# Top-k attention and Fourier mixing on one core: the second pair's q loaded before the tables and transposed in the third step

## The chip, the core and the metric

The kernel runs on one core of one Trainium2 chip. The core has five engines that run side by side, each through its own queue of instructions: TensorE (PE; its weight loads are shown apart as PEld), VectorE (DVE), ScalarE (ACT), GpSimd (POOL) and SyncE (SP), which here only issues transfers. The metric is the device time of one execution in microseconds, as a median over runs. A lower time is better.

## What is computed

Eight batches, each with eight heads of 576 rows and 64 channels. For each row of q the scores against all keys are formed, only the 32 largest are kept, and a softmax over these weighs v. The heads are put side by side to rows of 512 channels, a two-dimensional Fourier transform is added (its real part), the rows are normalised, and a two-layer MLP with a hidden width of 2048 is added.

```python
scores = scale * np.matmul(q, k.transpose(0, 1, 3, 2))
kth = np.partition(scores, -top_k, axis=-1)[..., -top_k:-top_k + 1]
attn = softmax(np.where(scores >= kth, scores, -1e9))
x = heads_side_by_side(np.matmul(attn, v))
u = x + np.real(fft(fft(x, axis=1), axis=2))
un = (u - mean(u)) / np.sqrt(var(u) + 1e-6)
out = u + np.maximum(un @ w_ch1, 0.0) @ w_ch2
```

## The kernel before

Two heads of one batch make a pair; there are 32 pairs, four for each batch. The rows of a pair are cut into nine tiles (four row blocks for each head, and one tile with the tails of both heads), so that there are 288 tiles, numbered 0 to 287, and 36 for a batch. The main loop (line 1049) makes one step for each tile. The order of the instructions on each engine is the order in which this Python program emits them; [...] each engine works through its own list.

In step i the loop emits, for the first batch:

- ACT conversion of a weight chunk (`scale_high`, line 171, and `rest`, lines 187 and 190). The weights arrive in a 64-bit form, 32 chunks of 512 KB, into five slots of one space, and are turned into 32-bit values by ACT, by DVE (`shift`, line 178) and by POOL (`join`, lines 197 and 198). Chunk n is converted in step n+1 (from chunk 16 on one step later), and the load of chunk n+5 into the slot that came free is issued by SP in the same step (line 165).
- ACT's exponent of tile i-1 (`expo`, line 390).
- PE's scores for the tiles ahead (`scores`, lines 346 and 316; ACT copies them to S at lines 349 and 320). A step handles the main part for two tiles or the tail part.
- In two steps of a pair's nine, the preparation of the next pair: `prep("q", ...)` or `prep("k", ...)`, five transposes on PE (line 260), and ACT copies to qT (268) or kT (270, 274). The natural rows come from `load_nat`, eight transfers issued by SP (lines 214 and 230: four of 64 KB and four of 8 KB).
- PE's transposes of tile i-1 (line 411 and, for its tail part, 422 or 426), which ACT copies to PT (414, 423), and for some tiles the product with v (448).
- DVE's search: four rounds of MAX8 (line 367) with three MATCH_REPLACE8 (369) for each tile. Step i does the last two rounds of tile i and the first two of tile i+1.
- POOL's threshold of tile i (`bounds`, line 376), ACT's mask (383), and POOL's subtraction (384). ACT's mask of tile i stands behind the PT copies of tile i-1 in ACT's list.
- DVE's shift of the weight chunk, then POOL's join of it.

q and k of all pairs but the first k share one buffer, `nat_t`. So the q of pair 1 may be loaded only when the q of pair 0 has been transposed, and the k of pair 1 only when the q of pair 1 has been. In the kernel before, q is prepared in the first step of a pair (i % 9 == 0) and k in the sixth (i % 9 == 5); the load of k follows in the step of q's preparation, and the load of the next q in that of k's.

Ahead of the loop, in this order, stand: the loads of the first q and k, the transposes of the first two row blocks of q and of all of k (lines 874 and 875), the loads of three weight chunks and of v, of the Fourier tables fs, fd and sg (895 to 897), of two more weight chunks, then the scores of tiles 0 and 1, the rest of the first q's transposes, the load of the second pair's q, and the scores of tiles 2 and 3. The tail part of tiles 2 and 3 is emitted there and again in step 0, with the same values.

From the second batch on, the MLP of the batch before fills PE beside the attention. The first batch has no such work beside it.

Of the kernel before, what the change touches and what calls it, by code (L numbers as in the profile page):

```python
# [64 lines left out]
def kernel(  # L65
# [15 lines left out]
    NC = 5  # L81
    NF = NC - 1
# [136 lines left out]
    def load_full(dst, src, pair):  # L219
        for e in range(2):  # L220
            for h in range(2):
                load_half(dst, src, pair, e, h)

    def load_tails(dst, src, pair, row0=(0, 0), queue=None, heads=(0, 1)):
        b, hp = divmod(pair, NPB)
        for e in heads:
            s2 = src[b, 2 * hp + e].rearrange("(h r) d -> h r d", h=2)
            for h in range(2):
                r0 = row0[e] + TH * h
                (queue or nc.sync).dma_start(  # L230
                    out=dst[r0:r0 + TH, NF, e, :], in_=s2[h, 2 * P:HS, :]
                )

    def load_nat(n, pair):
        if pair < NPAIR:
            nat[n, pair] = nat_t
            src = q if n == "q" else k
            load_full(nat[n, pair], src, pair)
            load_tails(nat[n, pair], src, pair)

    def load_v(pair):
        if pair < NPAIR:
            v_of[pair] = v_t[pair % 2]
            load_full(v_of[pair], v, pair)
            load_tails(v_of[pair], v, pair, (0, TAIL))

    def prep(n, pair, blocks=((0, NF), (NF, NC))):

        if pair >= NPAIR:
            return 0.0  # L250
        src, got_of = nat[n, pair], qT_of if n == "q" else kT_of
        if pair not in got_of:
            got_of[pair] = attp.tile(
                [P, S if n == "q" else NF * P], F32, name=f"{n}T_{pair}", tag=f"{n}T"
            )
        t_sb = got_of[pair]
        for c0, c1 in blocks:
            tp = ps_t.tile([P, 4, P], F32, name=f"tp{n}_{pair}_{c0}", tag="tp")
            for c in range(c0, c1):
                nc.tensor.transpose(  # L260
                    tp[:, c - c0, :], src[:, c, :, :].rearrange("p h d -> p (h d)"), ident
                )
            if c0 < NF:
                dst, got = t_sb[:, c0 * P:c1 * P], tp.rearrange("p a c -> p (a c)")[:, 0:(c1 - c0) * P]
            else:
                dst, got = t_sb[:, NF * P:], tp[:, 0, 0:TAIL]
            if n == "q":
                nc.scalar.mul(out=dst, in_=got, mul=scale)
            elif c0 < NF:
                nc.scalar.copy(out=dst, in_=got)  # L270
            else:
                for e in range(2):
                    r = slice(D * e, D * (e + 1))
                    nc.scalar.copy(out=kt_t[r, TAIL * e:TAIL * (e + 1)], in_=tp[r, 0, 0:TAIL])
        return 0.7
# [3 lines left out]
    PER_PAIR = len(IN_PAIR)  # L279
# [4 lines left out]
    N = len(items)  # L284
# [588 lines left out]
    nc.gpsimd.memset(ftail, 0.0)  # L873
    prep("q", 0, ((0, 2),))
    prep("k", 0)


    plan, costs, arrivals = {}, {}, []
# [11 lines left out]
    AHEAD = 5  # L890
    load, scale_high, shift, rest, join = weight_steps(wcs, sp1, WC, AHEAD)
    for n in range(3):
        load(n)
    load_v(0)
    nc.sync.dma_start(out=fs, in_=fs_d.ap())
    nc.sync.dma_start(out=fd, in_=fd_d.ap())
    nc.sync.dma_start(out=sg, in_=sg_d.ap())
    for n in range(3, AHEAD):
        load(n)
    start_of = [0] + [34 * n // len(wcs) for n in range(1, len(wcs))]  # L900
    for n, s0 in enumerate(start_of):
        at(s0 + 1, "convert", lambda n=n: scale_high(n))
# [121 lines left out]
    def run(i, where):  # L1024
        for fn in plan.pop((i, where), []):
            fn()
# [10 lines left out]
            got += one_unit()  # L1037
        return got

    for c in range(2):  # L1040
        scores(0, c)
    prep("q", 0, ((2, NF), (NF, NC)))
    load_nat("q", 1)
    for c in range(2):
        scores(2, c)
    for op in top_ops(0, (0, 1)):
        op()
    i, carry = 0, 0.0
    while i < N + 4 or plan or queue:
        now[0] = i  # L1050
        run(i, "begin")
        pair_of = i // PER_PAIR

        short = 0 <= i - 1 < PER_BATCH
        done = i - 1 if short else i - 2 if PER_BATCH <= i - 2 < N else None

        fixed, j = [], i + 3
        e = items[j][2] if j < N else None  # L1060
        preps = []
        if i < N and i % PER_PAIR == 0:
            preps.append(lambda: prep("q", pair_of + 1))
        if i < N and i % PER_PAIR == 5:
            preps.append(lambda: prep("k", pair_of + 1))
        fixed.append(lambda: scores(j - 1, 1) if e == 1 else scores(j, 0))
        n_mask = 0
        fixed += preps

        tok = []  # L1070
        if pending and pending[0][0] <= i:
            _, pp, pc = pending[0]
            if pp // NPB < 2 or pp // NPB - 2 in written:
                pending.pop(0)
                tok.append(lambda: to_tokens(pp, pc, not short))
        if not short:
            fixed += tok
        for where in ("pe1", "pe2", "pe"):
            fixed += plan.pop((i, where), [])
        if e is None and j < N:  # L1080
            fixed.append(lambda: scores(j, 1))
        n_tr = len(fixed)
        if done is not None:
            fixed.append(lambda: transposes(done))
        if short:
            fixed += tok
            pair, r = divmod(i - 1, PER_PAIR)
            piece = {1: (0, 0, P), 4: (0, P, CW[0]), 6: (1, 0, P), 8: (1, P, CW[1])}.get(r)
            if piece is not None:
                fixed.append(lambda: attend(pair, *piece))  # L1090
            if i == PER_BATCH:
                fixed.append(lambda: attended(NPB - 1, 1, late_next) or 0.0)
                fixed.append(lambda: to_tokens(NPB - 1, 1, False))
        if i in arrivals:
            carry = min(carry, 0.0) if i > arrivals[0] else -5.0
            run(i, "units")
            step_us = level(i)
        room = step_us - carry - fixed_cost(i)
        cost, got = carry, 0.0
        run(i, "convert")  # L1100
        if short:
            expo(i - 1)
        for n, fn in enumerate(fixed):
            cost += fn()
            if n == n_mask:
                if PER_BATCH <= i - 1 < N:
                    mask(i - 1)
                run(i, "act")
                for fn in out_next:
                    fn()  # L1110
                out_next.clear()
            if n == min(n_tr, len(fixed) - 1) and PER_BATCH <= i - 1 < N:
                expo(i - 1)

            got += some(max(room * (n + 1) / len(fixed) - got, 1.1 if fn in preps else 0.0))
        if short:
            if piece is not None and r in (4, 8) and i < PER_BATCH:

                out_next.append(lambda pc=(pair, r // 8): attended(*pc, late_next))
                pending.append((i + 1, pair, r // 8))  # L1120

        soon_tile = 2 * PER_BATCH - 1
        for tile in (i - 3, i - 2):
            if not PER_BATCH <= tile < N or (tile == i - 2) != (tile == soon_tile):
                continue
            pair, r = divmod(tile, PER_PAIR)
            if r in (4, 8):
                cost += attend(pair, r // 8)
                attended(pair, r // 8, late_next)
                pending.append((i + 1, pair, r // 8))  # L1130
        if i < N:
            if i % PER_PAIR == 0:
                load_nat("k", pair_of + 1)
            if i % PER_PAIR == 5:
                load_nat("q", pair_of + 2)
            if i % PER_PAIR == 6:
                load_v(pair_of + 1)
        first, second = top_ops(i, (2, 3)), top_ops(i + 1, (0, 1))
        for n in range(max(len(first), len(second))):
            for ops in (first, second):  # L1140
                if n < len(ops):
                    ops[n]()

        run(i, "pool0")
        bounds(i)
        if i < PER_BATCH:
            mask(i)
        for fn in late_now:
            fn()
        run(i, "dve")  # L1150
        for where in ("pool", "pool2", "load", "load2"):
            run(i, where)
        late_now[:] = late_next
        late_next.clear()
        carry = max(-4.0, min(4.0, cost + got - step_us))
        i += 1
# [36 lines left out]
```

## Time and profile before

| What | us |
|---|---|
| median of 8 runs | 1950.57 |
| lowest and highest of them | 1949.25 and 1951.54 |
| the profiled execution | 1950.67 |
| its span, from the first to the last instruction | 1948.9 |
| PE busy | 1826.7 (94%) |
| DVE busy | 1577.8 (81%) |
| ACT busy | 1202.8 (62%) |
| POOL busy | 773.9 (40%) |

The busy times are sums over the whole span. They hide that the kernel has stages: the page's row of 40 slices, 48.7 us each, has PE at 4 to 7 tenths in the first five slices and at 9 from the eighth on, and DVE at 9 or more in the second to the fourth. So the first 250 us have to be read by themselves. The granted clock of TensorE is a mean of 0.968 over the span, and 7 tenths in the first five slices.

In a line of the timeline, the first two numbers are the start and the length, in us; the bracket at its end tells how long the engine had been idle, and what ended the wait. SPq is SP's own queue: what is shown there is the issue of a transfer and not the transfer.

### The profile page before, as it was taken

The numbers are of one execution on the slowest core, as the hardware profiler recorded it, in microseconds if no ns is written. First come the engines' busy times: TensorE is split into PE (matmuls) and PEld (weight loads), VectorE is DVE, ScalarE is ACT, GpSimd is POOL, SyncE is SP. The second block draws the span as 40 slices with busy tenths as digits, with TensorE's granted clock in tenths as the row PEclk, the third lists the DMA queues.
The fourth block names the chain that finished last, engine by engine and source line by source line (L and its number), as shares of the span: only waits on it lengthen the run. The fifth ranks groups of instructions, "written<-read, shape, count | busy, mean of one in ns | idle before, by whom it ended". The sixth has DMA issues, their size and how long they took to land.

```text
span 1948.9 us, 27231 instructions
## 1 busy us (share of the span) xinstructions
PE 1826.7 (94%) x8626; PEld 1120.9 (58%) x8626; DVE 1577.8 (81%) x3245; ACT 1202.8 (62%) x3062; POOL 773.9 (40%) x1054
## 2 busy tenths in 40 slices
PE   4666699999999999999999999999999999998999
PEld 2443365464664756556664756556664756566655
DVE  7999989999999999888888879988888879843000
ACT  5878657776776767666666657666666657541100
POOL 3768642335523454235523444235522444232000
PEclk7777799999999999999999999999999999999999
DMA  4333100100001010010101100010001100000000
GB/s 144 108 94 106 29 13 20 32 20 24 23 16 29 21 30 13 19 33 19 24 19 25 27 22 18 16 32 19 24 19 25 27 22 20 1 14 1 11 14 11
DMA packets 133583, 57.80 MB, mean 30 GB/s; under 512 B 124352, under 2 KB 124480, under 8 KB 133440
## 3 DMA queue, kind: packets, MB, share of 16 engines
q1 hardware_dynamic: 132656, 55.85, 10.8%
q8 instruction: 69, 1.13, 0.3%
q14 instruction: 74, 0.61, 0.1%
q10 hardware_dynamic: 784, 0.21, 0.0%
HBM read 46.57 MB, written 9.44 MB: 29 GB/s over the span
## 4 chain that ended last, share of the span: by engine, by line
PE 78%; POOL 9%; DVE 5%; issue 4%; ACT 2%; DMA 1%; SPq 0%; ACTq 0%; POOLq 0%; DVEq 0%
PE hp L742 24%; PE cp L766 22%; PE o L448 7%; PE tpP L411 5%; PE sp L346 5%; POOL wk L384 3%; PE yp L607 3%; PE cp L802 3%; PE mp L656 2%; POOL w L198 2%; POOL w L197 2%; DVE m L367 2%; PE sp_t L316 2%; DVE wk L369 2%; PE tpq L260 1%
## 5 line engine op out<-in xcount | busy, mean ns | idle before, releaser
L384 POOL TENSOR_TENSOR wk<-S,wk 128x576 f32<-128x576 f32 x288 | 407.4, 1414 | 920.9 <-ACT wk L383 873.1
L367 DVE MAX8 m<-wk 128x8 f32<-128x576 f32 x864 | 623.3, 749 | 5.5
L742 PE MATMUL hp<-unT,w 128*128 128x256 f32 (+1 forms) x2048 | 538.8, 410 | 3.1 <-ACT unT L723 2.1
L766 PE MATMUL cp<-w,hT 128*128 128x512 f32 x1024 | 477.2, 597 | 0.0
L742 PEld LDWEIGHTS hp<-unT,w 128*128 128x128 f32 x2048 | 373.5, 191 | 126.1 <-issue 31.2
L369 DVE MATCH_REPLACE8 wk<-m,wk 128x576 f32<-128x576 f32 x576 | 427.5, 742 | 0.0
L766 PEld LDWEIGHTS cp<-w,hT 128*128 128x128 f32 x1024 | 179.4, 190 | 180.5 <-issue 179.9
L390 ACT ACTIVATE wk<-wk,nt 128x576 f32<-128x576 f32 x288 | 224.8, 781 | 53.6 <-POOL wk L384 52.7
L411 PE MATMUL tpP<-ident,wk 128*128 128x128 f32 x1152 | 183.9, 284 | 68.6 <-ACT wk L390 46.2
L414 ACT COPY PT<-tpP 128x512 f32<-128x512 f32 (+1 forms) x320 | 171.5, 548 | 117.9 <-PE tpP L411 115.5
L383 ACT ACTIVATE wk<-S,nt 128x576 f32<-128x576 f32 x288 | 227.0, 788 | 26.5 <-POOL nt L376 25.2
L411 PEld LDWEIGHTS tpP<-ident,wk 128*128 128x128 f32 x1152 | 139.9, 145 | 164.8 <-ACT wk L390 67.0
L746 ACT ACTIVATE hT<-hp 128x320 f32<-128x320 f32 (+1 forms) x256 | 104.9, 410 | 194.4 <-PE hp L742 192.0
L367 DVE MAX8 m<-S 128x8 f32<-128x576 f32 x288 | 214.0, 743 | 11.9 <-ACT S L320 11.6
L369 DVE MATCH_REPLACE8 wk<-m,S 128x576 f32<-128x576 f32 x288 | 213.6, 742 | 0.0
L448 PE MATMUL o<-PT,v 128*64 128x256 f32 (+3 forms) x1440 | 195.4, 415 | 2.2 <-ACT PT L414 1.6
L349 ACT COPY S<-sp 128x512 f32<-128x512 f32 (+1 forms) x264 | 141.9, 589 | 64.6 <-PE sp L346 64.4
L346 PE MATMUL sp<-kT,qT 64*128 64x512 f32 (+1 forms) x528 | 159.4, 666 | 4.3 <-ACT means L929 3.3
L448 PEld LDWEIGHTS o<-PT,v 128*64 128x64 f32 x1440 | 111.3, 153 | 76.1 <-issue 17.7
L780 DVE SCALAR_TENSOR_TENSOR x<-cp,gi,x 128x512 f32<-128x512 f32 x11 | 8.2, 746 | 128.3 <-PE cp L766 128.3
L316 PEld LDWEIGHTS sp_t<-kt,qT 128*128 128x128 f32 x322 | 56.2, 195 | 51.1 <-issue 20.1
L346 PEld LDWEIGHTS sp<-kT,qT 64*128 64x128 f32 (+1 forms) x528 | 42.1, 189 | 61.7 <-issue 44.3
(126 smaller groups left out, 1821.5 us busy)
## 6 DMA issues: line engine op xcount, KB each, us to landing
space<-in_moe_w_ch_dram SPq DMA_DIRECT2D x32, 512.0 KB, 3.6
nat<-in_q_dram SPq DMA_DIRECT2D x128, 64.0 KB, 2.1
v<-in_v_dram SPq DMA_DIRECT2D x128, 64.0 KB, 2.1
out_dram<-x SPq DMA_DIRECT2D x32, 256.0 KB, 2.1
nat<-in_k_dram SPq DMA_DIRECT2D x124, 64.0 KB, 2.2
nat<-in_q_dram SPq DMA_DIRECT2D x128, 8.0 KB, 1.8
v<-in_v_dram SPq DMA_DIRECT2D x128, 8.0 KB, 1.8
nat<-in_k_dram SPq DMA_DIRECT2D x124, 8.0 KB, 1.7
```

The lines of the kernel that those rows point to most:

```text
L346: nc.tensor.matmul(sp[r], lhsT=qT[hd, q_cols], rhs=kT[hd, :], start=True, stop=True)
L349: nc.scalar.copy(out=s_t[r, keys], in_=sp[r])
L367: ops.append(lambda src=src, m8=m8: nc.vector.max(out=m8, in_=src))
L369: ops.append(lambda src=src, m8=m8: nc.vector.match_replace(w, m8, src, NEG))
L383: nc.scalar.activation(out=w, in_=Ssb[i], func=AF.Relu, scale=-FAR, bias=Nt[i][:, 1:2])
L384: nc.gpsimd.tensor_tensor(out=w, in0=Ssb.pop(i), in1=w, op=ALU.subtract)
L390: nc.scalar.activation(out=w, in_=w, func=AF.Exp, bias=Nt.pop(i)[:, 0:1], accum_out=den_t[pair % 3][:, c:c + 1],)
L411: nc.tensor.transpose(tp[:, c, :], p_sb[:, k0 + P * c:k0 + P * (c + 1)], ident)
L414: nc.scalar.copy(out=pt[:, NF * he:NF * (he + 1), col:col + w], in_=tp[:, :, o:o + w])
L448: nc.tensor.matmul(o[D * e:D * (e + 1), c0:c1], lhsT=vv[:, c, e, :], rhs=pt[:, 2 * NF if c == NF else NF * e + c, c0:c1], start=(c == 0), ...
L742: nc.tensor.matmul(hp[:, 0:w], lhsT=w1[:, dt, P * it:P * (it + 1)], rhs=unT[:, dt, 0:w], start=(dt == 0), stop=(dt == NDT - 1),)
L766: nc.tensor.matmul(cp, lhsT=hT[:, it, P * n:P * (n + 1)], rhs=w2[:, it, :], start=(it == 0), stop=(it == NIT - 1),)
```

## The change

Four things are done. The scores of tiles 0 and 1, the rest of the first q's transposes and the main scores of tiles 2 and 3 are emitted ahead of the weight loads in the program. The second pair's q is loaded right after v, ahead of weight chunks 3 and 4, and these go ahead of the tables. The tail scores of tiles 2 and 3, emitted twice before, are emitted only in step 0. For pair 0 alone, the preparation of the next q moves from step 0 to step 2, and the load of the next k with it. All later pairs stay as they were.

```diff
     prep("q", 0, ((0, 2),))
     prep("k", 0)
+    for c in range(2):
+        scores(0, c)
+    prep("q", 0, ((2, NF), (NF, NC)))
+    scores(2, 0)
...
     for n in range(3):
         load(n)
     load_v(0)
+    load_nat("q", 1)
+    for n in range(3, AHEAD):
+        load(n)
     nc.sync.dma_start(out=fs, in_=fs_d.ap())
     nc.sync.dma_start(out=fd, in_=fd_d.ap())
     nc.sync.dma_start(out=sg, in_=sg_d.ap())
-    for n in range(3, AHEAD):
-        load(n)
...
-    for c in range(2):
-        scores(0, c)
-    prep("q", 0, ((2, NF), (NF, NC)))
-    load_nat("q", 1)
-    for c in range(2):
-        scores(2, c)
     for op in top_ops(0, (0, 1)):
         op()
...
-        if i < N and i % PER_PAIR == 0:
+
+        q_step = i == 2 if pair_of == 0 else i % PER_PAIR == 0
+        if i < N and q_step:
             preps.append(lambda: prep("q", pair_of + 1))
...
         if i < N:
-            if i % PER_PAIR == 0:
+            if q_step:
                 load_nat("k", pair_of + 1)
```

In the lists of the engines this does the following. On SP, the eight issues of the second q pass two weight loads and the three table loads, and the eight issues of the second k fall behind the load of weight chunk 5. On PE, the five transposes of the second q move from ahead of the scores of tile 4 to behind the main scores of tiles 5 and 6 (step 2), and one tail matmul goes. On ACT, the two qT copies move from ahead of the mask of tile 0 to between the S copies and the PT copies of step 2, and two S copies go. On DVE, the memset of `ones` (line 909) falls behind the copies of the first tails (line 320), ahead of the first MAX8. POOL's list is the same.

## The prediction

> **What bounds the kernel now.** I read the busy shares of the 40 slices first, then a table by stage, then the chain of waits at the start, then the timeline of 10 to 42 us engine by engine.
>
> The table by stage (stretch, its length, then for each engine busy us and instructions, granted TensorE clock, DMA share, GB/s):
>
> ```profile
> 10.00:24.00 14.00, 3.08 (x12) 1.44 (x11) 13.27 (x27) 2.32 (x9) 0.19 (x1) 0.66 0.87 294
> 24.00:41.00 17.00, 12.53 (x54) 6.83 (x52) 13.73 (x27) 14.54 (x32) 9.39 (x9) 0.58 0.18 49
> 41.00:125.00 84.00, 49.10 (x262) 32.47 (x261) 83.14 (x171) 70.94 (x167) 59.45 (x60) 0.77 0.40 116
> 330.00:1949.00 1619.00, 1592.80 (x7479) 972.71 (x7477) 1277.66 (x2627) 968.10 (x2493) 587.39 (x840) 1.00 0.08 21
> ```
>
> The order is PE, PEld, DVE, ACT, POOL. From 330 us PE is busy 1592.80 of 1619 us and sets the end; before that the first batch has no MLP beside it, and VectorE is full (83.14 of 84 us). All hand-overs are between engines, so the PE stage starts when the first batch lets it, and a shift of the first batch should arrive at the end whole.
>
> The chain of waits, its pieces around 20 us (start, length, what):
>
> ```profile
> 17.59 5.97 DMA nat<-in_q_dram
> 23.55 0.14 issue
> 23.69 1.10 PE tpq L260 x4
> 24.81 0.71 ACT qT L268 x2
> 25.52 0.67 ACT wk L383
> 26.20 0.07 issue
> 26.26 1.42 POOL wk L384
> ```
>
> So the last arrival at the start is the second pair's q, and behind it runs a POOL chain that the trace follows, almost unbroken, from 26 to 221 us. The timeline gives the price (start, length, engine, operation, idle before it and its releaser):
>
> ```profile
> 16.64 2.31 SPq L214 DMA_DIRECT2D nat<-in_q_dram  x4
> 17.00 0.19 POOL L376 TENSOR_TENSOR nt<-m,cc 128x2 f32<-128x2 f32 x1 [15.06 <-DVE m L367]
> 24.81 0.71 ACT L268 ACTIVATE qT<-tpq 128x512 f32<-128x512 f32 x2 [10.95 <-PE tpq L260]
> 25.41 0.78 ACT L383 ACTIVATE wk<-S,nt 128x576 f32<-128x576 f32 x1
> 26.07 0.63 ACT L171 ACTIVATE wh<-space 128x512 f32<-128x512 f32 x1
> 26.26 1.42 POOL L384 TENSOR_TENSOR wk<-S,wk 128x576 f32<-128x576 f32 x1 [9.07 <-ACT wk L383]
> 26.74 0.69 DVE L178 TENSOR_SCALAR w<-wh 128x512 int32<-128x512 int32 x1 [3.23 <-ACT wh L171]
> 31.28 0.78 ACT L383 ACTIVATE wk<-S,nt 128x576 f32<-128x576 f32 x1
> ```
>
> The threshold of tile 0 (L376) stood ready at 17.2, but its mask (L383) was behind the qT copies on ACT, which waited 10.95 us for transposes, which waited for q. VectorE lost 3.23 us at L178 for the same reason, and twice 0.23 us in the next steps (32.61, 39.76).
>
> **What the Trainium skill says.** "TensorE: Matmul & The Clock Gate", section Architectural detail, calls ACT and DVE strict FIFO: one waiting instruction holds all behind it. The trace agrees (ready at 17.2, ran at 25.41). "DMA: Bandwidth & Descriptors", section Issuing engines are not separate DMA queues, says that all issues end on the same 16 engines and interleave; here they are 0.87 busy from 10 to 24 us, so an earlier place in line is worth something. The first page's Part 1 gives a free-running 3413 ns window in which PE is granted full or half rate; the stage rows agree as far as they can (0.58, 0.77, 1.00 as means).
>
> **The change part by part.** The profiled execution took 1950.67 us, its span 1948.9, with 1.77 around it; the median of the eight runs is 1950.57. I work against 1950.67.
>
> 1. SP queue. Ahead of q stood v, fs, fd, sg and two weight chunks; now only v. SP ended v's issues at 13.75 and needs no wait on PE there: q's old buffer was read by 10.4. Eight issues at about 0.45 us end near 17.4. q landed at 23.55 after about 4.2 MB had been asked for since 7 us; now about 2.1 MB stands before its end, at the stage's 294 GB/s some 7 us, so 15 to 20 us. It is first needed in the third step, near 25. fs, fd and sg serve the DFT after 220 us; weight chunks 3 and 4 are converted in steps 4 and 5. All of these cost nothing. k of pair 1 is now issued after weight chunk 5, which waits for the join of chunk 0 (L198). By part 4 below that ends at 28.1; eight k issues run from 28.6 to 32.2, landing near 34.5 (median 2.2 us). The k transposes, at 46.10 before, would be due at 39.6: 5 us spare. If q came late, PE's list would stop at its transposes, and with it the transposes of tile 1, ACT's PT copies and mask 2: the wait that is there now, two steps on; the spare there is 5 us or more.
>
> 2. Removed: the second pass of the tail scores of tiles 2 and 3 (one matmul, two ACT copies of 0.33 us together). ACT was idle then (10.95 us): nothing.
>
> 3. The memset of ones (0.17 us, at 1.56 before) now stands in front of the first MAX8 on DVE. Nothing hides it: +0.15.
>
> 4. ACT and POOL. Threshold of tile 0 at 17.00+0.15; mask 0.22 later (as 41.21 to 41.43): 17.37 instead of 25.41, 8.0 earlier. Chunk 0 landed at 13.45, so the conversion that follows doesn't wait; scores of tile 4 are on PE at about 13.5. Mask to mask was 5.87 (25.41 to 31.28), so mask 1 is at 23.24; its threshold (VectorE's fourth MAX8 of tile 1, done at 22.0+0.15) is ready. Subtract 0.85 later, then 1.42+1.26+1.29 to the end of L198: 28.1. The third step now carries the q preparation. Mask 1 to the S copies 3.10 (31.28 to 34.38): 26.34; copies 1.06: 27.40; qT copies until the transposes run 0.64 and from there to the mask 1.79, both as in step 18 (123.57, 124.21, 126.00): mask 2 at 29.83, not 36.36. The gain is 6.5; 1.5 of the 8.0 went on the preparation in a busy ACT.
>
> 5. Does it last? From tile 2 to 17 the POOL chain is its own pace: L384, L197, L198, threshold and ACT's mask, 5.07 us a step, or 6.4 where ACT is late. It lags VectorE: threshold start less the end of the tile's last MAX8 is 5.3 us at tile 2, 3.0 at tiles 9, 13 and 17, 2.5 at 14 (whose mask had 1.4 us to spare). VectorE moves up by 3.23+0.23+0.23-0.15 = 3.54 only, and has no gap from 41 to 125 us. So the POOL chain can gain 3.54+2.96 = 6.5 before VectorE holds it: the two limits meet. VectorE recovers the rest later: between 135 and 156 us it idled 0.78+1.18+0.55+0.55 = 3.06 us for PE and ACT, which will come earlier, so the gap of 3.0 between the chains closes there.
>
> 6. From 156 us on all engines are about 6.5 earlier, through the DFT into the PE stage; nothing there waits for a transfer.
>
> Sum: 6.5, less 0.2 for the places where both chains now meet: 6.3. 1950.67-6.3 = 1944.4; from the median, 1944.3.
>
> **Unknown costs.** The placement of q's preparation in step 3: at best its 0.71 us of copies fill ACT's idle 0.26 us of that step and cost 0.45 (gain 7.5, which VectorE caps at 6.5); at worst PE's five transposes (1.38 us at 23.69) stand in the path too, 2.5 in all (gain 5.5). I take 1.5, from step 18. PE's granted clock: a half-rate window of 3.4 us costs up to 1.7 us where PE sets the pace; one more or one fewer is 1.7 either way, and the eight runs lie within 2.3, so I allow one.
>
> **Rivals.**
> A. VectorE alone decides: the first batch is VectorE-bound and its later idle pieces stay. For it: 83.14 of 84 us busy. Against it: those pieces end with ACT and PE, which are on the earlier chain. Gain 3.54: 1947.1, within the bound of no change.
> B. The gain is hidden: something later, a store, a weight load or the DFT's tables, comes at its own time. Against it: no DMA is in the chain after 23.55, and DMA is at 0.05 to 0.4 of its engines. About 1950.
> C. Slower, by PE's clock. Place: 24 to 250 us, where PE has short bursts, and its transposes stand between ACT's exponent and ACT's next mask. Price: four transposes took 0.66 us at full and 1.12 at half rate, a whole half-rate window at most 1.7. For it: the change spreads PE's early work otherwise, and the clock in 41 to 125 us is at 0.77, so it can fall. Point: from 4 windows more (6.8) the gain is gone; with 6 more (10.2) it is slower by 3.9 us: 1954.5. Against it: nothing in these steps changes the pattern after step 3.
> That k comes late in step 5 would also lengthen the path, but only from a landing after 46.1, 11.6 us later than worked out.
>
> **How the numbers follow.** The measurement can tell 0.2% (3.9 us) from no change. Forecast (gain 4 to 8.5) 0.76; A 0.15; B 0.04; C 0.05. The predicted time is the forecast's. Its own range is 1942.2 to 1946.6; taking in A and half-way to B gives 1942.2 to 1948.3. Faster 0.76; same 0.18 (A, B, and nearly all of what lies between B and C's end point); slower 0.06.
>
> **What would show it.** In the new trace: SP issues q right after v, landing near 18 to 20; no 3.23 us before the first L178; the first L383 near 17.4, the third L384 near 30.7 (37.21 before); q transposes near 25 to 27 with no DMA wait; k transposes without a DMA wait near 40; L384 of tile 17 near 114.6 (121.11), and L178 at 137.24 with its 1.18 us wait gone; the DFT's token stage (L607, 245.6) near 239. It would be wrong if the third L384 is less than 5 us earlier, if VectorE holds L376 in steps 9 to 17, or if the 135 to 156 us pieces remain on VectorE.

## The result, and the profile after

| | before | changed |
|---|---|---|
| median | 1950.67 (28 runs, 1949.23 to 1954.95) | 1943.57 (10 runs, 1942.69 to 1945.35) |
| span of the profiled execution | 1948.9 | 1941.8 |
| start of the threshold (L376) of tile 17 | 120.02 | 113.47 |
| first matmul of the DFT (L607) | 245.55 | 239.20 |

The ratio is 0.9965, with a 95% interval of 0.9957 to 0.9973: 7.1 us faster by the medians (5.3 to 8.4 by the interval), where 6.3 were forecast.

The table by stage of the changed kernel, with the columns of the one shown before (the first two stretches are cut at the same times, so they hold more of the work now):

```profile
10.00:24.00 14.00, 7.12 (x22) 2.93 (x20) 13.76 (x29) 8.00 (x20) 1.88 (x4) 0.80 0.70 227
24.00:41.00 17.00, 9.94 (x54) 6.53 (x52) 16.90 (x35) 15.07 (x33) 13.12 (x13) 0.80 0.50 155
41.00:125.00 84.00, 53.15 (x277) 34.86 (x278) 83.14 (x171) 69.89 (x167) 58.42 (x58) 0.75 0.37 107
```

VectorE (the third pair of numbers) is full from 10 us on: 13.73 of 17 us have become 16.90 of 17 in the second stretch. From 41 us on it was full before and is full now (83.14 of 84 us in both): its work there is not less, it only begins earlier. The timeline of the changed kernel around the old stall:

```profile
15.10 1.92 SPq L214 DMA_DIRECT2D nat<-in_q_dram  x4
17.20 0.78 ACT L383 ACTIVATE wk<-S,nt 128x576 f32<-128x576 f32 x1 [3.62 <-POOL nt L376]
18.05 1.42 POOL L384 TENSOR_TENSOR wk<-S,wk 128x576 f32<-128x576 f32 x1 [0.89 <-ACT wk L383]
22.05 0.19 POOL L376 TENSOR_TENSOR nt<-m,cc 128x2 f32<-128x2 f32 x1 [2.58 <-DVE m L367]
22.59 0.58 ACT L414 COPY PT<-tpP 128x512 f32<-128x512 f32 x1 [0.43 <-PE tpP L411]
23.07 0.78 ACT L383 ACTIVATE wk<-S,nt 128x576 f32<-128x576 f32 x1
23.40 0.68 DVE L178 TENSOR_SCALAR w<-wh 128x512 int32<-128x512 int32 x1
24.50 1.15 PE L260 MATMUL tpq<-ident,nat 128*128 128x128 f32 x5
29.99 1.43 POOL L384 TENSOR_TENSOR wk<-S,wk 128x576 f32<-128x576 f32 x1 [1.88 <-ACT wk L383]
```

The mask of tile 0 (L383 at 17.20) follows its threshold (16.97) by 0.23 us, and ACT is now the one that waits for POOL. The first L178 has no bracket: its 3.23 us are gone. The transposes of q at 24.50 wait for no transfer. The third subtraction is at 29.99, not 37.21. The chain of waits has changed its beginning (pieces around 20 us; two of 0.02 us at 23.9 are left out; start, length, what):

```profile
18.44 1.41 DVE m L367 x2
19.85 1.46 DVE wk L369 x2
21.30 0.68 DVE m L367
21.98 0.07 issue
22.05 0.19 POOL nt L376
22.24 1.65 issue
23.93 1.43 POOL wk L384
```

VectorE's search stands where the transfer of q stood, but at tile 1 it is not what held the mask: the threshold was ready at 22.24, and the mask ran at 23.07, behind ACT's copy of PT at 22.59, which had waited for PE. The view has that time as "issue". VectorE comes into the chain again further on; the same view from 81 us:

```profile
81.07 1.32 DVE m L367 x2
82.39 1.46 DVE wk L369 x2
83.84 0.68 DVE m L367
84.52 0.07 issue
84.59 0.19 POOL nt L376
```

In the kernel before, the chain followed POOL through this whole stretch; now POOL waits for the last MAX8 of tile 12 at 84.6 us, and for that of tile 13 at 90.1, and ACT's mask comes right behind:

```profile
90.14 0.19 POOL L376 TENSOR_TENSOR nt<-m,cc 128x2 f32<-128x2 f32 x1 [0.43 <-DVE m L367]
90.37 0.78 ACT L383 ACTIVATE wk<-S,nt 128x576 f32<-128x576 f32 x1 [0.39 <-POOL nt L376]
```

### The profile page after: what moved, and what is told of

It is laid out like the page before. It is cut to its first block, busy times and chain, and to the rows that moved or that the text cites. A ratio compares the mean times of both kernels' runs of the same rounds, so it can differ in the third digit from the quotient of the medians.

```text
span 1941.8 us, 27224 instructions
## 1 busy us (share of the span) xinstructions
PE 1826.1 (94%) x8624; PEld 1121.1 (58%) x8624; DVE 1577.2 (81%) x3245; ACT 1201.2 (62%) x3060; POOL 773.2 (40%) x1054
## 4 chain that ended last, share of the span: by engine, by line
PE 78%; POOL 8%; DVE 6%; issue 4%; ACT 3%; DMA 0%; SPq 0%; POOLq 0%; DVEq 0%; ACTq 0%
PE hp L742 24%; PE cp L766 22%; PE o L448 7%; PE tpP L411 5%; PE sp L346 5%; PE yp L607 3%; PE cp L802 3%; POOL wk L384 3%; DVE m L367 3%; PE mp L656 2%; DVE wk L369 2%; POOL w L198 2%; POOL w L197 2%; PE sp_t L316 2%; PE tpk L260 1%
## 5 line engine op out<-in xcount | busy, mean ns | idle before, releaser
L383 ACT ACTIVATE wk<-S,nt 128x576 f32<-128x576 f32 x288 | 227.0, 788 | 30.8 <-POOL nt L376 29.6
```

Source lines behind the costliest of these rows:

```text
L383: nc.scalar.activation(out=w, in_=Ssb[i], func=AF.Relu, scale=-FAR, bias=Nt[i][:, 1:2])
```

## The experiments

In all of them, "gain at tile 17" is how much earlier than in the profile of the kernel before the threshold of tile 17 (L376) started. It shows the first batch apart from what PE's clock does later, in the one execution that was profiled. Each time is a median, beside that of the kernel before measured together with it; these medians of the kernel before differ by up to 1.6 us, so a run is set against its own.

| run | time | before | ratio (95% interval) | gain at tile 17 |
|---|---|---|---|---|
| changed kernel | 1943.57 | 1950.67 | 0.9965 (0.9957 to 0.9973) | 6.6 |
| preparation moved only | 1943.78 | 1950.46 | 0.9966 (0.9953 to 0.9978) | 6.7 |
| transfers moved only | 1944.90 | 1950.46 | 0.9970 (0.9959 to 0.9981) | 6.3 |
| the remaining parts | 1950.74 | 1950.46 | 1.0000 (0.9992 to 1.0008) | 0.3 |
| before, VectorE loaded | 1954.46 | 1951.15 | 1.0018 (1.0012 to 1.0025) | -4.1 |
| changed, VectorE loaded | 1949.92 | 1951.15 | 0.9992 (0.9984 to 1.0001) | 0.4 |
| before, POOL loaded | 1953.13 | 1951.15 | 1.0006 (0.9998 to 1.0015) | -1.2 |
| changed, POOL loaded | 1946.04 | 1951.15 | 0.9972 (0.9961 to 0.9983) | 6.2 |
| changed, q in step 1 | 1943.86 | 1951.57 | 0.9966 (0.9954 to 0.9978) | 6.9 |
| changed, q in step 4 | 1944.63 | 1951.57 | 0.9966 (0.9953 to 0.9978) | 6.8 |
| changed, conversions later | 1942.73 | 1952.04 | 0.9956 (0.9942 to 0.9969) | 7.8 |

**The parts of the change.** First the preparation alone, on the kernel before:

```diff
-        if i < N and i % PER_PAIR == 0:
+        q_step = i == 2 if pair_of == 0 else i % PER_PAIR == 0
+        if i < N and q_step:
             preps.append(lambda: prep("q", pair_of + 1))
...
-            if i % PER_PAIR == 0:
+            if q_step:
                 load_nat("k", pair_of + 1)
```

> The preparation of the second q moves to step 2 (and with it the load of its k), the transfers keep their old order. My theory: what cost time was mask 0 standing behind q on ACT, so this alone gives the whole gain: q lands near 23.5 as before, its transposes are reached near 24.5, without a wait; third L384 near 30, 1943.5 to 1944.5. Rival (the early place of q in SP's queue does it): q still lands too late, the wait moves to step 2 with it, gain under 2 us.

It gives nearly the whole gain (6.7 of 7.1 us, with intervals that overlap). The timeline has q's transposes of this run without a wait, though q is asked for as late as before (issues at 17.42 to 24.0 us):

```profile
24.57 1.09 PE L260 MATMUL tpq<-ident,nat 128*128 128x128 f32 x5
```

So q's old place on SP was early enough for step 2. Then the transfers alone: the changed kernel with the preparation back in step 0.

```diff
-        q_step = i == 2 if pair_of == 0 else i % PER_PAIR == 0
+        q_step = i % PER_PAIR == 0
```

> The new order of transfers with the preparation left in step 0. My theory: q lands near 20.8, mask 0 follows 1.9 us later near 22.6 instead of 25.4: the POOL chain gains 2.8, VectorE's wait at the first L178 falls from 3.2 to about 0.5; 1947.5, a gain of 2.5 to 3.3. Rival (early q is what counts): a gain of 6 to 7, 1944.

Both theories missed: the gain is 5.6 us (3.7 to 8.0 by the interval), twice what I expected, and the profile has the reason. PE's transposes of q, from the timeline of this run:

```profile
17.57 0.66 PE L260 MATMUL tpq<-ident,nat 128*128 128x128 f32 x2 [4.59 <-DMA nat<-in_q_dram]
18.50 0.66 PE L260 MATMUL tpq<-ident,nat 128*128 128x128 f32 x2 [0.27 <-DMA nat<-in_q_dram]
19.81 0.45 PE L260 MATMUL tpq<-ident,nat 128*128 128x128 f32 x1 [0.65 <-DMA nat<-in_q_dram]
```

q came in pieces and PE took each as it landed, so four of five transposes were done before the last piece. That piece was there at 19.8, not 20.8, and mask 0 followed 0.6 us later, at 20.42, where I had taken 1.9 from the kernel before, whose five transposes all ran after the landing. Mask 0 is 5.0 us earlier, and not 2.8; VectorE lost nothing (its first L178 needs ACT's conversion by 23.4). From 5.0 at tile 0 the gain grew to 6.3 at tile 17. Each of the two parts takes away nearly the same wait, and they don't add. The third run has neither:

```diff
     load_v(0)
-    load_nat("q", 1)
-    for n in range(3, AHEAD):
-        load(n)
...
     nc.sync.dma_start(out=sg, in_=sg_d.ap())
+    for n in range(3, AHEAD):
+        load(n)
+    load_nat("q", 1)
...
-        q_step = i == 2 if pair_of == 0 else i % PER_PAIR == 0
+        q_step = i % PER_PAIR == 0
```

> Only the scores ahead of the loads in the program and the doubled tail scores left out; transfers and preparation as before. My theory: nothing, 1950.7 within 0.8. Rival (the removed matmul and copies or the memset's new place count): more than 1 us either way.

Nothing: 0.3 us by the medians, and within 1.6 us either way by the interval. The doubled tails, the place in the program and the memset are worth no time that these runs can show.

**Which chain is the bound.** Step 5 of the prediction has two chains, VectorE's and POOL's with ACT, and says that POOL's was 3 us behind and that the two meet now. Work was added to one or the other, in both kernels. On VectorE, memsets that write the values that are there already:

```diff
+    def pad():
+        for _ in range(24):
+            nc.vector.memset(ones, 1.0 / DM)
+
+    at(3, "dve", pad)
```

> The kernel before with 24 more memsets of ones on VectorE at the end of step 3, some 2.2 us of work by 0.09 each (the trace will tell how much). Theory of two chains: in the kernel before the POOL chain is 2.5 to 5 us behind VectorE in the steps up to 17, so VectorE has that much to spare: it costs 0 to 0.4. Rival (VectorE alone sets the first batch): the whole 2.2.

> The changed kernel with the same memsets. Theory of two chains: VectorE holds the thresholds now from step 11 on, nothing is to spare: it costs 1.7 to 2.2. Rival (the POOL chain is still the only bound): 0 to 0.5.

The memsets were longer than I took them for. The timeline of the changed kernel with them (the kernel before has the same 6.11):

```profile
34.56 0.68 DVE L178 TENSOR_SCALAR w<-wh 128x512 int32<-128x512 int32 x1
35.21 6.11 DVE L917 MEMSET ones<- 128x128 f32 x24
46.14 0.68 DVE L178 TENSOR_SCALAR w<-wh 128x512 int32<-128x512 int32 x1
```

With 6.0 us in place of 2.2 the sizes have to be worked out again, after the run. In the changed kernel the threshold of tile 17 went from 113.47 to 119.63, by 6.2, and the end by 5.9, when each kernel is set against its own kernel before: all of it is paid. In the kernel before, VectorE moved back by 5.7 (0.3 fell into an idle piece), but the threshold of tile 17 by 2.8 only, when the 1.3 us are taken off by which that profile was late from its first step, and the time by 3.3 (2.3 to 4.9 by the interval). So VectorE had 2.9 us to spare before, against 2.96 read from the trace, and none now. Tile 14 agrees: with the 2.51 us read there, 5.7 on VectorE should have cost 3.2, and its threshold was 3.3 later. On POOL:

```diff
+    def pad():
+        for _ in range(4):
+            nc.gpsimd.memset(ftail, 0.0)
+
+    at(3, "pool", pad)
```

> The kernel before with four memsets of ftail (0.52 each, 2.1 us in all) on POOL at the end of step 3. Theory of two chains: POOL is the bound, so it costs the whole 2.1. Rival (VectorE alone sets the first batch): 0 to 0.5.

> The changed kernel with the same POOL memsets. Theory of two chains: the chain was 7.2 us ahead at the third L384 but only 6.5 at the eighteenth, so 0.7 is to spare: it costs 1.2 to 1.6. Rival (VectorE alone is the bound now): 0 to 0.5.

These took 2.28 us. In the kernel before, the next threshold was 2.2 later, that of tile 17 by 0.7 and that of tile 34 by 2.1, when the 0.4 us are taken off by which that profile was late from its start; the end was 2.0 later by medians (an interval of -0.4 to 2.9). In the changed kernel the next threshold was 2.5 later, that of tile 17 by 0.4, that of tile 34 by 1.6, and the end by 2.0 against its own kernel before. These two runs don't decide between the theories: part of the size is lost in what PE's clock does to this chain. Tile 10 shows how: in the trace of before, then of the changed kernel, the scores of the tail tile that ACT waits for:

```profile
77.41 1.97 PE L346 MATMUL sp<-kT,qT 64*64 64x512 f32 x4
```

```profile
70.20 1.07 PE L346 MATMUL sp<-kT,qT 64*64 64x512 f32 x4
```

The same four matmuls took 1.97 and 1.07 us, at a granted clock of 0.50 and 1.00, and the subtraction of the tile that follows stood 6.9 and 5.7 us after the one ahead of it. Here that is worth 1.2 us of the POOL chain. The kernel before with POOL loaded gained the same 1.2 us at this tile, so its loss shrank there though nothing that bounds the chain had changed. The changed kernel with POOL loaded got 1.1 us back at tiles 12 and 13, where VectorE holds the changed kernel and, by the trace, not this one: there the two chains do show.

**Where the preparation may stand.** On the changed kernel, step 1 or step 4 in place of step 2:

```diff
-        q_step = i == 2 if pair_of == 0 else i % PER_PAIR == 0
+        q_step = i == 1 if pair_of == 0 else i % PER_PAIR == 0
```

> The changed kernel with q's preparation in step 1, not 2. Theory of two chains: PE meets q's transposes near 15 and stands until q lands near 19.8, mask 1 comes about 1 us later than in the changed kernel, but step 2 has no preparation then, so mask 2 is at 29.2 again; threshold of tile 17 within 0.5 us of the changed kernel, 1943.0 to 1944.5. Rival (the third step is what makes the change work): the stand of PE in step 1 costs 2 us or more.

> The changed kernel with q's preparation, and so the load of k behind it, in step 4. Theory: the load of k then stands on SP behind weight chunk 7, which waits for the join of chunk 2 near 39.1; k lands near 45, some 5 us after step 5 wants its transposes (39.6), PE and ACT stand for it, and the POOL chain loses 4 to 5 us there, of which 0 to 1 is made up later: 1946.5 to 1948. Rival (k has slack or VectorE covers it): under 1 us, 1944.

Step 1 does as well as step 2, as expected: mask 1 was 0.7 us later than in the changed kernel and mask 2 was 0.3 earlier. Step 4 did not cost what I said. k was late, and PE waited for it:

```profile
42.81 1.09 PE L260 MATMUL tpk<-ident,nat 128*128 128x128 f32 x4 [2.88 <-DMA nat<-in_k_dram]
```

That is 2.9 us, not 5: the first pieces of k were there at 42.8, and PE takes k in pieces too. The POOL chain's gain fell from 7.9 at tile 3 to 5.3 at tile 7, as it should. But at tile 17 it was 6.8. In the changed kernel the chain reaches 8.0 at the threshold of tile 11 and is then held by VectorE at tiles 12 and 13, down to 6.9; the chain that lost 2.6 us early comes to these tiles with 6.5 and is held at neither. So most of an early loss was paid by waits that the chain would have had anyway. Not all of it: at tile 34 the gain was 5.8, against 6.3 in the changed kernel. The medians, each against its own kernel before, are 6.9 and 7.1 and can't tell the two apart.

**Beyond the change.** If VectorE is the limit anywhere in steps 1 to 17, less of its work there should help a little. Weight chunks 0 to 15 are converted one step later, which leaves none in step 1:

```diff
-    start_of = [0] + [34 * n // len(wcs) for n in range(1, len(wcs))]
+    start_of = [n + 1 if n < n1 else 34 * n // len(wcs) for n in range(len(wcs))]
```

> The changed kernel with weight chunks 0 to 15 converted one step later each (steps 2 to 17, where step 17 had none): the same work, but none of it in step 1. Theory of two chains: VectorE is 0.6 us earlier from step 1 to 17 (one shift) and ACT and POOL are about 2 us earlier there, but VectorE has its sixteenth shift back in step 17 and holds the threshold of tile 18 as now; ACT's mask 18 has 1.2 us over that threshold, so the end of the first batch gains 0 to 1: 1942.6 to 1943.6. Rival (the conversions in the first step are what holds the chains): 2 us or more, 1941.5.

1942.73 is the lowest median here, but its interval of the ratio overlaps with the changed kernel's, and that execution began its first threshold 0.5 us earlier than the profile of the kernel before, for no reason that the program shows. By the ratios the gain over the change would be 1.8 us; neither that nor nothing is excluded.

## Why the prediction was right

The direction and the cause are shown: each of the two moves that end the wait for q brings most of the gain by itself, and the run without both brings none. The size was within 0.8 us, in part because errors of opposite sign met in step 5. By its steps:

1. SP's queue. q was issued from 15.10 and not 13.75, because SP reached v 0.5 us later and its last four issues took 3.96 us, where the four like them of q took 1.80: by the trace SP stood there for the landing of weight chunks (two waits, 2.4 us). q still landed before 24.5. k's issues began at 28.43 (28.6 worked out), and its transposes at 38.89 met no wait. That the new transfer order costs nothing is right; that it is not needed is what the prediction did not say. It priced the landing and the move of the preparation as one thing; the runs with one part each show them as two cures for one wait.
2. Removed tails: nothing that the third run could show.
3. The memset in front of the first MAX8: 0.15 was too much. The MAX8 started at 10.11, against 10.09, so the memset cost 0.02.
4. ACT and POOL: mask 0 at 17.20 (17.37 worked out), mask 1 at 23.07 (23.24), mask 2 at 29.13 (29.83), the third subtraction at 29.99 (30.7). The preparation cost 1.0 and not 1.5: PE's transposes of tile 1 behind it took 0.66 us, where the row I took it from, in step 18, had 1.12.
5. The two limits. VectorE came 4.0 us earlier, not 3.54. Of the difference 0.15 is the memset, which cost next to nothing; the rest is that each of the three stalls cost about 0.1 more than its idle time, since two operations that follow at once overlap by about that much (the shift after the first stall moved by 3.34 where 3.23 was idle). The sum of lag and VectorE's gain holds where VectorE is the limit: at tile 13 it gives 4.0+3.0 = 7.0, less the 0.08 us that the threshold takes to follow, and the gain there is 6.9. So the limit was 6.9 us and not the 6.5 worked out. The threshold of tile 17 was due at 113.5 and came at 113.47 all the same, because the chain lost another 0.3 at the mask of tile 15, where the scores that ACT waits for took PE 1.54 us and not 1.22, at a granted clock of 0.71 where it had been 0.93: that the two meet so closely is luck. One of the prediction's signs of being wrong came true: VectorE does hold L376 at tiles 12 and 13. That sign stood against the prediction's own step 5, which has VectorE take over when POOL's chain has gained its lag; by the loaded runs the step is right, and the sign was badly chosen. Of the 3.06 us of idle pieces between 135 and 156 us, only one of 0.52 is left (148.78, the old 155.20).
6. Into the PE stage: the DFT was due near 239 and began at 239.20. The gain of the thresholds is 6.3 at tile 34 and stays 6.3 to 6.4 as far as tile 80, so the forecast sum is what the mechanism brings as far as there.

The other 0.8 of the two profiled executions is PE's clock. Between tiles 80 and 90 the gain goes to 8.1; the granted clock in the stretch of 30 us around it, before and then after, is the number ahead of the last two:

```profile
480.00:510.00 30.00, 24.50 (x130) 16.83 (x129) 26.21 (x55) 19.75 (x53) 17.32 (x21) 0.89 0.07 19
```

```profile
474.00:504.00 30.00, 24.51 (x138) 16.39 (x136) 26.98 (x58) 21.37 (x58) 19.38 (x24) 0.94 0.07 19
```

The record of the granted clock in these traces has only full and half rate, and its half-rate pieces are 3.41 us long or a whole multiple of that, but for the one that the end cuts. The kernel before has two of them in this stretch (from 485.54 and 499.20 us), the changed one has one (from 479.30): 3.41 us at half rate are worth 1.7 us of PE, which is the step from 6.4 to 8.1. After 1750 us the changed kernel gives about 1 us back in the same way (two pieces against one; 0.83 against 0.91 in a stretch of 20 us). The ten runs of the changed kernel have mean clocks from 0.967 to 0.972, so such pieces seem to come and go between runs of one kernel; only one run of each kernel has a profile, so this is not shown piece by piece. The prediction allowed for one of them.

Of the rivals, A (VectorE alone decides) falls with the loaded run of the kernel before, where 5.7 us on VectorE cost half. B falls, since nothing held the gain back. C did not happen: the mean clock from 41 to 125 us is 0.75 against 0.77, which is 1.7 us less of full rate in 84 us, about one piece where C needed more than four.

## What to carry to other kernels

A transfer that comes late costs what stands behind its consumer in the list of an engine that works in order, here ACT. Moving the consumer down the list can do as much as moving the transfer up, and the two don't add (6.7 and 5.6 us alone, 7.1 together). Before giving a price to such a wait, read how far a second chain lags behind the first: the gain is at most the smaller of what the waiting chain wins and what the other one wins plus that lag. A loss early in the waiting chain can cost less than its own length, when a wait for the other chain further on would have taken that time in any case.

## What was not expected

That PE would use q in pieces was not expected: q comes in eight transfers, and the landing of the last one says little about when the work on it can start. And a memset of 128x128 on VectorE took 0.25 us in a row of 24 (6.11 us in all), though the first ones of the kernel show 0.17; no run here shows why.
